# Whole-array transposes for the first four groups, two 64-row tiles for all other groups, and a rewritten work order

## The chip, the core and the metric

The kernel runs on one core of a Trainium2 chip. The metric is the device time of one execution in microseconds (us), lower is better. The engines are TensorE (PE, matrix products; its weight loads are listed apart as PEld), VectorE (DVE), ScalarE (ACT), GpSimd (POOL) and SyncE (SP, which here issues the transfers). Matrix products and transposes write to PSUM banks; the other engines read these.

## The reference, cut to what matters

`x` is 4 batches of 12480 tokens with 128 channels, `inducing` 32 rows of 128, the weights are 128 x 2048 and 2048 x 128, all float32.

```python
def mab(q, kv):
    s = scale * (q @ kv.transpose(0, 2, 1))
    s = s - s.max(-1, keepdims=True)
    a = np.exp(s)
    a /= a.sum(-1, keepdims=True) + 1e-09
    return a @ kv
h = mab(I, x)                       # 32 inducing rows attend to the tokens
attn = mab(x, h)                    # the tokens attend to the 32 rows of h
hid = attn.reshape(49920, 128) @ w_in
out = np.maximum(0.01 * hid, hid) @ w_out
```

## The kernel before

The tokens of a batch are cut into six groups of 2048 and a rest group of 192 (g = 6). A group's rows lie in SBUF as 128 partitions with 16 tokens each (`xr`, 1 MB, six buffers). Two passes run over the groups of each batch.

The first pass: LD loads a group; T (`turn`, L1711) transposes it on PE, from SBUF into PSUM, and C (`turned`, L1734) copies the four results to `xT` on ACT or DVE; S1 forms the 32 scores of each token; E takes their maxima and a copy; after two groups (a step: 0 and 1, 2 and 3, 4 to 6) RD, X and NM combine the maxima; W takes the exponentials on ACT, Y transposes them on DVE in blocks of 32; V is the value product on PE, with `xr` as its moving operand, after which `xr` is free for a later load; GA adds the steps up. After the third step ZP, RZ, HS, HP and HC make the transposed hidden state `hT`. H, HT, SH, G, FO, FC, SP and SC then fold both weight matrices and the leak into one matrix of 32 rows for the batch (`folded`).

The second pass of the same batch: S2 forms scores with `hT`, LO, LE and U make weights of them, and O, the output product, uses `folded`. SA, RC, D and DM divide by the sums, ST stores. The second pass of a batch is woven into the first pass of the next. The weights arrive in eight blocks of 0.5 MB (LW), each converted from 64 to 32 bits by CA and CT on ACT, CB and CO on DVE and CP on POOL.

What order each engine works in is written out by hand in the table `ORDER`: every token stands for one call, the letter at its end is the engine (a for ACT, v for DVE, p for POOL), the digit behind @ a PSUM bank. Each engine runs its own instructions in the order of this table and waits for others only where data or a buffer need it. SP issues all loads and stores of the table in order, too.

A transpose before the change comes in two forms. The groups in `EARLY` (all six of batch 0 and the first three of batch 1) are turned in one visit in four tiles of 32 rows, 64 PE passes with 32 columns each, into both pairs of banks (`po0`, `po1`) that the output products use later. The other fifteen are turned in two visits in two tiles of 64 rows, 16 passes with 64 columns each, into two single banks. The rest group is turned whole, in two passes with 96 rows.

Of the kernel before, what the change touches and what calls it, by code (L numbers as in the profile page):

```python
# [1383 lines left out]
class Plan:  # L1384
# [3 lines left out]
        LD0.0.0 LD0.0.1 T0.0.0 C0.0.2a C0.0.3a C0.0.0v C0.0.1v LD0.1.0 T0.1.0 C0.1.0a C0.1.1a C0.1.3v C0.1.2v LW0  # L1388
        CT0 CB0 S10.0@0 S10.1@1 CA0 E0.0 CO0 CP0 LD0.2.0 LD0.3.0 LD0.4.0 T0.2.0 C0.2.0a C0.2.1a C0.2.3a C0.2.2a LW1
        E0.1 RD0.0 X0.0@2 NM0.0 W0.1 W0.0 T0.3.0 C0.3.2v C0.3.0a C0.3.1a C0.3.3v Y0.0 Y0.1 S10.2@3 CA1 CB1 CT1 CO1  # L1390
        CP1 LW2 CA2 T0.4.0 C0.4.3a C0.4.2a C0.4.0a C0.4.1a V0.0@0 S10.3@1 LD0.5.0 V0.1 E0.2 CB2 CT2 CO2 CP2 ZT0.0
        E0.3 RD0.1 LW3 CB3 CA3 LW4 LD0.6.0 LD1.0.0 LD1.1.0 T0.5.0 C0.5.2v C0.5.0a C0.5.1a C0.5.3v S10.4@2 X0.1@3
        NM0.1 CO3 T0.6.0@1 C0.6.0v E0.4 S10.5@3 E0.5 CA4 AL0.1 S10.6@1 E0.6 RD0.2 CB4 CO4 CT3 CP3 CT4 W0.3 W0.2 CP4
        T1.0.0 C1.0.2a C1.0.1a C1.0.0a X0.2@2 NM0.2 AL0.2 W0.5 Y0.3 Y0.2 V0.2@3 V0.3 ZT0.1 Y0.5 GA0.0 W0.4 Y0.4
        C1.0.3a W0.6 ZT0.2 Y0.6 LW5 LW6 CA5 GA0.1 T1.1.0 C1.1.3a C1.1.2a C1.1.1a CA6 C1.1.0a CT5 CB5 CO5 CP5 ZP0@1
        RZ0 CB6 V0.4@2 V0.5 V0.6 GA0.2 HS0 CO6 CT6 CP6 S11.0@0 E1.0 HP0@3 HC0 LW7 CB7 S11.1@1 E1.1 CA7 CO7 RD1.0 CT7
        CP7 H0.0@2 HT0.0 SH0.0 S20.0@0 X1.0@3 NM1.0 LO0.0 LE0.0 LD1.2.0 LD1.3.0 T1.2.0 T1.3.0@12 C1.3.1v C1.2.1a
        C1.3.0a C1.2.2a U0.0 C1.2.3a C1.2.0a S20.1@3 G0.0p FO0.0@1 FC0 T1.3.1@20 C1.3.2v C1.3.3a LO0.1 LE0.1 S20.2@1
        W1.0 Y1.0 SP0@0 SC0 W1.1 U0.1 S11.2@2 E1.2 LO0.2 O0.0.0.0 SA0.0.0.0a O0.0.0.1 SA0.0.0.1a D0.0.0.0a RC0.0.0
# [958 lines left out]
```

## Time and profile before

| | before |
|---|---|
| time, median of 3 runs | 199.67 us (198.2 to 202.84) |
| the profiled execution's own time | 198.97 us |
| span from first to last instruction | 197.2 us |
| PE busy | 169.0 us (86%), 3471 products and 3471 weight loads |
| DVE busy | 146.6 us (74%) |
| ACT busy | 127.6 us (65%) |
| POOL busy | 89.8 us (46%) |
| DMA | 55.93 MB, 284 GB/s over the span |
| granted PE clock, mean | 0.913 of 2.4 GHz |

A timeline row gives the start in us from the beginning of the span, the time from the group's first start to its last end, the engine, the line of the kernel, the operation, output<-input, the shapes and how many instructions were merged into the row; in brackets stands how long the engine stood idle just before it and what ended the idle time. "issue" is idle time in which the engine waited for nothing that the profile shows. A granted clock of 1.00 is 2.4 GHz, 0.50 is 1.2 GHz. PE passes of float32 operands count double in the rows of products, single in the rows of transposes.

### The profile page before, as it was taken

How to read it: one execution, taken by the hardware profiler on the slowest of the kernel's cores; microseconds unless marked ns; L12 is line 12 of the kernel's file. 1: busy time of each engine (PE TensorE's matmuls, PEld its weight loads, DVE VectorE, ACT ScalarE, POOL GpSimd, SP SyncE). 2: the span in 40 equal slices, each digit the busy share in tenths (PEclk: the TensorE clock that was granted, in tenths of full speed). 3: DMA queues.
4: the chain of work that ended last, by engine and by line, in shares of the span. 5: the costliest groups of instructions: out<-in, count | busy, mean ns of one | idle time of the engine just before them, and what ended most of it. 6: DMA issues, size and time to landing. Idle time of an engine off the chain costs nothing.

```text
span 197.2 us, 8331 instructions
## 1 busy us (share of the span) xinstructions
PE 169.0 (86%) x3471; PEld 109.2 (55%) x3471; DVE 146.6 (74%) x461; ACT 127.6 (65%) x336; POOL 89.8 (46%) x96
## 2 busy tenths in 40 slices
PE   7596988698799999979889999799999978898930
PEld 2546664573438586766437578345683673465710
DVE  2361869859497978969659898587978879988950
ACT  2247659864697976964649986558996843666410
POOL 2010132208227386760156655284294654788640
PEclk9955589699999999999999999999999999999555
DMA  6999879599403999998995559999846353397992
GB/s 201 369 419 424 313 277 412 180 294 407 178 3 106 396 357 383 406 385 285 354 370 217 216 179 352 381 384 344 332 177 258 118 185 132 132 315 283 380 371 72
DMA packets 19357, 55.93 MB, mean 284 GB/s; under 512 B 1104, under 2 KB 3312, under 8 KB 16368
## 3 DMA queue, kind: packets, MB, share of 16 engines
q1 hardware_dynamic: 19056, 55.22, 75.3%
q8 instruction: 28, 0.46, 1.0%
q10 hardware_dynamic: 256, 0.11, 0.3%
q14 instruction: 17, 0.14, 0.2%
HBM read 29.77 MB, written 25.56 MB: 281 GB/s over the span
## 4 chain that ended last, share of the span: by engine, by line


## 5 line engine op out<-in xcount | busy, mean ns | idle before, releaser
L2052 POOL TENSOR_TENSOR osb<-stage,inv 128x512 f32<-128x512 f32 (+1 forms) x75 | 75.1, 1019 | 55.7 <-DVE inv L2033 18.8
L1741 ACT COPY xT<-xT_ps 128x512 f32<-128x512 f32 x66 | 36.7, 601 | 26.2 <-PE xT_ps L1729 26.0
L2004 PE MATMUL po<-folded,uT 32*128 32x129 f32 (+1 forms) x792 | 42.8, 302 | 2.8 <-ACT uT L1984 0.9
L2045 ACT COPY stage<-po 128x512 f32<-128x512 f32 (+1 forms) x75 | 41.5, 581 | 4.4 <-PE po L2004 4.3
L2004 PEld LDWEIGHTS po<-folded,uT 32*128 32x128 f32 (+1 forms) x792 | 32.2, 189 | 21.5 <-ACT stage L2045 7.6
L1729 PE MATMUL xT_ps<-ident,xr 32*128 32x32 f32 (+1 forms) x1056 | 36.1, 242 | 6.9 <-issue 3.2
L1729 PEld LDWEIGHTS xT_ps<-ident,xr 32*128 32x128 f32 (+1 forms) x1056 | 30.8, 157 | 19.2 <-issue 10.7
L1843 PE MATMUL h_ps<-xr,ay 128*32 128x128 f32 x768 | 27.0, 291 | 2.3 <-DVE z L1826 2.3
L1749 PE MATMUL s_ps<-xT,indT 128*32 128x512 f32 x192 | 27.6, 662 | 0.3 <-ACT cv_a L1684 0.3
L1741 DVE COPY xT<-xT_ps 128x512 f32<-128x512 f32 x30 | 19.9, 682 | 10.6 <-PE xT_ps L1729 10.6
L1749 PE MATMUL s_ps<-xT,hT 128*32 128x512 f32 x192 | 26.4, 599 | 1.6 <-issue 1.3
L1843 PEld LDWEIGHTS h_ps<-xr,ay 128*32 128x32 f32 x768 | 22.4, 117 | 4.3 <-issue 2.7
L2026 ACT ACTIVATE inv<-po 128x4 f32<-128x4 f32 (+1 forms) x75 | 11.4, 175 | 19.3 <-PE po L2004 18.8
L1984 ACT ACTIVATE uT<-s_ps,least 128x512 f32<-128x512 f32 (+1 forms) x28 | 18.2, 650 | 4.4 <-DVE least L1968 4.2
L1959 DVE TENSOR_REDUCE low<-s_ps 128x1 f32<-128x512 f32 (+1 forms) x28 | 17.1, 609 | 3.5 <-PE s_ps L1749 3.4
L1770 DVE TENSOR_SCALAR_CACHE_REDUCE e<-s_ps 128x512 f32<-128x512 f32 (+1 forms) x28 | 17.1, 614 | 3.0 <-PE s_ps L1749 2.1
L1812 ACT ACTIVATE e<-e,nm 128x512 f32<-128x512 f32 (+1 forms) x28 | 18.9, 679 | 0.7 <-DVE nm L1796 0.7
L2047 DVE TENSOR_TENSOR osb<-po,inv 128x512 f32<-128x512 f32 (+2 forms) x29 | 18.0, 629 | 1.2
L1709 POOL TENSOR_TENSOR w_in_sb<-cv_a,cv_t 128x512 int32<-128x512 int32 x4 | 5.2, 1288 | 26.7 <-DVE cv_a L1694 21.0
L1821 DVE STREAM_TRANSPOSE ay<-e 128x512 f32<-128x512 f32 (+1 forms) x28 | 17.0, 621 | 0.0
L2033 DVE RECIPROCAL inv<-inv 128x8 f32<-128x8 f32 (+1 forms) x52 | 9.9, 191 | 2.0
L1709 POOL TENSOR_TENSOR w_out_sb<-cv_a,cv_t 128x512 int32<-128x512 int32 x4 | 5.3, 1324 | 10.6 <-ACT cv_t L1700 8.2
(95 smaller groups left out, 147.1 us busy)
## 6 DMA issues: line engine op xcount, KB each, us to landing
xr<-in_x_dram SPq DMA_DIRECT2D x23, 1024.0 KB, 8.1
out_dram<-osb SPq DMA_DIRECT2D x21, 1024.0 KB, 5.8
out_dram<-osb SPq DMA_DIRECT2D x6, 512.0 KB, 4.2
raw<-in_moe_w_in_dram SPq DMA_DIRECT2D x4, 512.0 KB, 14.1
raw<-in_moe_w_out_dram SPq DMA_DIRECT2D x4, 512.0 KB, 4.7
xr<-in_x_dram SPq DMA_DIRECT2D x2, 512.0 KB, 4.2
xrr<-in_x_dram SPq DMA_DIRECT2D x4, 96.0 KB, 6.7
out_dram<-osb SPq DMA_DIRECT2D x3, 96.0 KB, 4.9
```

Of the source, the lines that this page charges most:

```text
L1729: nc.tensor.matmul(V["T", b, g, j][:, n * k : n * k + n], xr[b, g][part, 8 * q + k, :], ident[part, part], is_transpose=True, tile_positio ...
L1741: copying(engine)(xT[b, g][:, n * at : n * at + n], V.pop(("T", b, g, j))[:, :n])
L1749: nc.tensor.matmul(ps[32 * j : 32 * j + 32, :w].rearrange("p (k r) -> p k r", r=32), lhsT, tokens[:, :, 32 * j % n : 32 * j % n + 32], sta ...
L1770: nc.vector.tensor_scalar(out=e[:rows], in0=V.pop(("S", b, g))[:rows, :w], scalar1=1.0, scalar2=None, op0=ALU.mult, op1=ALU.max, accum_out ...
L1812: nc.scalar.activation(e[:rows, :w], e[:rows, :w], AF.Exp, bias=nms[b, p][:rows], scale=SCALE, accum_out=zg[:rows])
L1843: nc.tensor.matmul(hp[32 * (k % 4) : 32 * (k % 4) + 32, :], t[:rows, k, :], rows_in[:rows, k, :], start=(i == 0 and k < 4), stop=(last[k % ...
L1959: V["latest", "DVE"] = nc.vector.tensor_reduce(out=low[:rows], in_=V["S2", b, g][:rows, :w], op=ALU.max, axis=AX.X, apply_absolute_value=T ...
L1984: V["latest", "Activation"] = nc.scalar.activation(dst, src, AF.Exp, bias=least[:rows, b, g : g + 1])
L2004: V["latest", "PE"] = nc.tensor.matmul(po[:m, j % 2, (P + 1) * i : (P + 1) * (i + 1)], uT[b, g][part, columns], folded[b % 2][part, :], st ...
L2045: nc.scalar.copy(raw[:m, :nj, :n], src)
L2047: nc.vector.tensor_tensor(out=dst, in0=src, in1=inverse_of(b, g, h, t)[4], op=ALU.mult)
L2052: V["latest", "Pool"] = nc.gpsimd.tensor_tensor(out=dst, in0=raw, in1=inv, op=ALU.mult)
```

## The change

The groups 0 to 3 of batch 0 (`WHOLE`) are turned by the whole array: four visits of four passes with 128 rows and 128 columns each, one bank a visit, two visits to a pair. All other big groups are turned in two visits in two 64-row tiles, those in `EARLY` into one bank pair a visit, the rest as before. The first load, which is cut in two pieces, lets the first two visits start on its first piece. Scores read `xT` with another stride for the whole groups. `ORDER` is written anew throughout; two planning costs change with it and don't reach the program.

```diff
-        LD0.0.0 LD0.0.1 T0.0.0 C0.0.2a C0.0.3a C0.0.0v C0.0.1v LD0.1.0 T0.1.0 C0.1.0a C0.1.1a C0.1.3v C0.1.2v LW0
+        LD0.0.0 T0.0.0 T0.0.1 C0.0.1v LD0.0.1 LD0.1.0 LD0.2.0 LD0.3.0 T0.0.2 C0.0.0v T0.0.3 C0.0.2a C0.0.3a T0.1.0
...
     EARLY = [(0, g) for g in range(NG)] + [(1, g) for g in range(3)]
+    WHOLE = [(0, g) for g in range(4)]
     PIECES = {(0, 0): 2}
-    T_FOUR, T_TWO = 0.85, 0.45
+    T_WHOLE, T_TWO = 0.437, 0.52
...
-        parts = range(4) if (b, g) in EARLY else range(2 * q, 2 * q + 2)
+        whole = (b, g) in WHOLE
+        n, parts = (P, [q]) if whole else (64, [2 * q, 2 * q + 1])
         for j in parts:
             if (b, g) not in EARLY:
                 V["T", b, g, j] = one_ps("xT_ps")
...
-        n = 32 if (b, g) in EARLY else 64
         for k in range(TOK // n):
             for i, j in enumerate(parts):
                 part = slice(n * i, n * i + n)
                 nc.tensor.matmul(
-                    V["T", b, g, j][:, n * k : n * k + n], xr[b, g][part, 8 * q + k, :], ident[part, part],
+                    V["T", b, g, j][:, n * k : n * k + n],
+                    xr[b, g][part, (4 if whole else 8) * q + k, :], ident[part, part],
                     is_transpose=True, tile_position=(n * i, 0),
                 )
...
-        at = j if (b, g) in EARLY else 2 * (j % 2) + j // 2
+        at = j if g == RG or (b, g) in WHOLE else 2 * (j % 2) + j // 2
...
-            n = rows if g == RG else 32 if (b, g) in EARLY else 64
-            at = 0 if g == RG else w * j if (b, g) in EARLY else 2 * w * (j // 2)
+            n = rows if g == RG or (b, g) in WHOLE else 64
+            at = 2 * w * (32 * j // n)
...
-        visits, tiles = (1 if early or not big else 2), (4 if big else 1)
+        whole = (b, g) in WHOLE
+        visits, tiles = (4 if whole else 2 if big else 1), (4 if big else 1)
...
-            banks = [("po0", "T", b, g), ("po1", "T", b, g)] if early else [("ps", "T", b, g, j) for j in js]
+            banks = [(f"po{js[0] // 2}", "T", b, g)] if early else [("ps", "T", b, g, j) for j in js]
```

PE's order at the start of the program, before: `busy_ps` is a warm-up, `xT_ps` a turn, `s_ps` a score product, `mx_ps` the combined maxima of a step, `h_ps` a value product (x16 is one group).

```order
L1655 MATMUL ind_ps<-ident,ind 128x32
L1729 MATMUL xT_ps<-ident,xr 128x32 x128
L1749 MATMUL s_ps<-xT,indT 32x512 x8
L1729 MATMUL xT_ps<-ident,xr 128x32 x64
L1598 MATMUL mx_ps<-rd,e_77 32x8 x4
L1729 MATMUL xT_ps<-ident,xr 128x32 x64
L1749 MATMUL s_ps<-xT,indT 32x512 x4
L1729 MATMUL xT_ps<-ident,xr 128x32 x64
L1843 MATMUL h_ps<-xr,ay 32x128 x16
L1749 MATMUL s_ps<-xT,indT 32x512 x4
```

The same place on PE in the changed kernel.

```order
L1657 MATMUL ind_ps<-ident,ind 128x32
L1731 MATMUL xT_ps<-ident,xr 128x128 x32
L1752 MATMUL s_ps<-xT,indT 32x512 x4
L1731 MATMUL xT_ps<-ident,xr 128x128 x16
L1752 MATMUL s_ps<-xT,indT 32x512 x4
L1731 MATMUL xT_ps<-ident,xr 128x128 x16
L1600 MATMUL mx_ps<-rd,e_77 32x8 x4
L1752 MATMUL s_ps<-xT,indT 32x512 x4
L1731 MATMUL xT_ps<-ident,xr 128x64 x16
L1752 MATMUL s_ps<-xT,indT 32x512 x4
L1731 MATMUL xT_ps<-ident,xr 128x64 x16
L1846 MATMUL h_ps<-xr,ay 32x128 x32
```

A group of 64 passes has become one of 16 (group 4 of 32), turns and scores alternate from the first group on, the score of group 3 and the second half of group 4's turn stand ahead of the first value product, and the first two value products stand together.

DVE's order from the maxima of step 2 of batch 0 on, before: `e,rm` are the maxima of a group, `cv_b` and `cv_a` sign and join of a weight block, `ay` the transposed exponentials that a value product needs, `lower,nm` a step's minimum.

```order
L1770 TENSOR_SCALAR e,rm<-s_ps 96x64
L1779 TENSOR_TENSOR rd<-rm,own 128x12
L1688 TENSOR_SCALAR cv_b<-raw 128x512
L1694 SCALAR_TENSOR_TENSOR cv_a<-cv_a,cv_b 128x512
L1798 TENSOR_SCALAR lower,nm<-mx_ps,nm 128x12
L1821 STREAM_TRANSPOSE ay<-e 128x512 x2
```

The same place on DVE in the changed kernel.

```order
L1773 TENSOR_SCALAR e,rm<-s_ps 96x64
L1773 TENSOR_SCALAR e,rm<-s_ps 128x512
L1782 TENSOR_TENSOR rd<-rm,own 128x12
L1824 STREAM_TRANSPOSE ay<-e 128x512 x2
L1801 TENSOR_SCALAR lower,nm<-mx_ps,nm 128x12
L1690 TENSOR_SCALAR cv_b<-raw 128x512
L1696 SCALAR_TENSOR_TENSOR cv_a<-cv_a,cv_b 128x512
L1690 TENSOR_SCALAR cv_b<-raw 128x512
L1696 SCALAR_TENSOR_TENSOR cv_a<-cv_a,cv_b 128x512
```

The two transposes have moved ahead of the weight block and of the minimum.

SP's order at the start, before: `xr` is a load of x, `raw` a weight block.

```order
L1670 DMA xr<-in_x_dram 128x1024 x2
L1670 DMA xr<-in_x_dram 128x2048
L1675 DMA raw<-in_moe_w_in_dram 128x1024
L1670 DMA xr<-in_x_dram 128x2048 x3
L1675 DMA raw<-in_moe_w_in_dram 128x1024 x2
```

The same place on SP in the changed kernel.

```order
L1672 DMA xr<-in_x_dram 128x1024 x2
L1672 DMA xr<-in_x_dram 128x2048 x3
L1677 DMA raw<-in_moe_w_in_dram 128x1024
L1672 DMA xr<-in_x_dram 128x2048
L1677 DMA raw<-in_moe_w_in_dram 128x1024
```

The first weight block has moved behind the loads of groups 2 and 3, and the second and third no longer go out together.

## Rows read from the trace of the kernel before

**Rows 1.** The page: busy us (share, count) of each engine; granted clock in 40 slices.

```profile
PE 169.0 (86%) x3471; PEld 109.2 (55%) x3471; DVE 146.6 (74%) x461; ACT 127.6 (65%) x336; POOL 89.8 (46%) x96
...
PEclk9955589699999999999999999999999999999555
```

**Rows 2.** Busy time by stage: us from:to, length, busy per engine, clock, DMA share, GB/s.

```profile
9.30:26.40 17.10, 15.50 (x313) 9.96 (x313) 10.02 (x21) 10.74 (x22) 2.58 (x2) 0.51 0.94 376
26.40:36.60 10.20, 6.82 (x210) 4.50 (x205) 7.98 (x28) 7.84 (x19) 3.85 (x3) 0.99 0.92 345
...
56.30:181.00 124.70, 116.90 (x2392) 75.40 (x2391) 103.39 (x337) 90.55 (x256) 71.06 (x72) 1.00 0.75 274
```

**Rows 3.** Timeline of PE in the opening.

```profile
5.17 1.42 PE L1729 MATMUL xT_ps<-ident,xr 32*128 32x32 f32 x64
8.71 1.92 PE L1729 MATMUL xT_ps<-ident,xr 32*128 32x32 f32 x64 [2.12 <-DMA xr<-in_x_dram]
10.55 3.64 PE L1749 MATMUL s_ps<-xT,indT 128*32 128x512 f32 x16
14.13 1.92 PE L1729 MATMUL xT_ps<-ident,xr 32*128 32x32 f32 x64
...
17.21 0.32 PE L1729 MATMUL xT_ps<-ident,xr 32*128 32x32 f32 x2 [0.94 <-ACT xT L1741]
18.19 1.92 PE L1729 MATMUL xT_ps<-ident,xr 32*128 32x32 f32 x62 [0.66 <-ACT xT L1741]
...
40.09 1.18 PE L1729 MATMUL xT_ps<-ident,xr 32*128 32x32 f32 x64
41.21 0.24 PE L1598 MATMUL z_ps<-zn,e 128*32 128x1 f32 x8
...
56.33 0.74 PE L2004 MATMUL po<-folded,uT 32*128 32x129 f32 x16
```

**Rows 4.** Timeline of PE: the rows that began after an issue gap.

```profile
29.20 0.49 PE L1729 MATMUL xT_ps<-ident,xr 32*128 32x32 f32 x18 [0.49 <-issue]
...
53.98 0.34 PE L1729 MATMUL xT_ps<-ident,xr 64*128 64x64 f32 x4 [1.42 <-issue]
...
99.11 1.05 PE L1749 MATMUL s_ps<-xT,hT 128*32 128x512 f32 x3 [1.29 <-issue]
...
124.39 0.52 PE L1729 MATMUL xT_ps<-ident,xr 64*128 64x64 f32 x9 [1.25 <-issue]
...
161.99 0.42 PE L1598 MATMUL floor_ps<-ident,floor 128*32 128x128 f32 x8 [1.05 <-issue]
```

**Rows 5.** DMA queues (packets, MB, share): page; 51.5 to 54; 26.5 to 29.5 us.

```profile
q8 instruction: 28, 0.46, 1.0%
...
q8 instruction: 1, 0.02, 2.9%
...
q8 instruction: 1, 0.02, 2.1%
```

**Rows 6.** Timeline of PE: a 64-row visit and the turn of a rest group.

```profile
64.81 0.71 PE L1729 MATMUL xT_ps<-ident,xr 64*128 64x64 f32 x16
65.45 0.38 PE L1716 MATMUL xT_ps<-ident,xrr 96*128 96x96 f32 x2
65.76 1.06 PE L1749 MATMUL s_ps<-xT,hT 128*32 128x512 f32 x8
```

**Rows 7.** Timeline of DVE and PE: from step 2's maxima to the hidden state.

```profile
33.74 0.42 DVE L1688 TENSOR_SCALAR cv_b<-raw 128x512 int32<-128x512 int32 x1
...
34.26 0.69 DVE L1694 SCALAR_TENSOR_TENSOR cv_a<-cv_a,cv_b 128x512 int32<-128x512 int32 x1
...
35.02 1.30 DVE L1821 STREAM_TRANSPOSE ay<-e 128x512 f32<-128x512 f32 x2
...
36.47 3.69 PE L1843 MATMUL h_ps<-xr,ay 128*32 128x128 f32 x64 [2.34 <-DVE z L1826]
...
44.30 0.32 PE L1598 MATMUL hT_ps<-folds,hc 128*32 128x64 f32 x8
```

More of the change, by code (lines that the diff above doesn't have):

```diff
@@ L1469 @@
+        DM3.5.1.1 ST3.3 ST3.4.0 ST3.4.1 ST3.5.0 ST3.5.1 END@0 SA3.6.0.0v O3.6.0.1 SA3.6.0.1v RC3.6.0 D3.6.0.0v
+        D3.6.0.1v SI3.6 ST3.6
     """
@@ L2129, in last_of @@
         b, g = (b, g - 1) if g else (b - 1, NG)
-        parts = {"LD": (PIECES.get((b, g), 1) - 1,), "T": (0 if g == RG or (b, g) in EARLY else 1,), "O": (0 if g == RG else 1, 1)}
+        parts = {"LD": (PIECES.get((b, g), 1) - 1,), "T": (0 if g == RG else 3 if (b, g) in WHOLE else 1,), "O": (0 if g == RG else 1, 1)}
         return [(kind, b, g, *parts.get(kind, ()))]
@@ L2148, in first_pass @@
         early = (b, g) in EARLY
-        visits, tiles = (1 if early or not big else 2), (4 if big else 1)
+        whole = (b, g) in WHOLE
+        visits, tiles = (4 if whole else 2 if big else 1), (4 if big else 1)
         for q in range(visits):
             js = range(tiles * q // visits, tiles * (q + 1) // visits)
-            banks = [("po0", "T", b, g), ("po1", "T", b, g)] if early else [("ps", "T", b, g, j) for j in js]
-            add(("T", b, g, q), {"PE": (T_FOUR if early else T_TWO) if big else 0.175}, lambda _, q=q: turn(b, g, q), mode="R" if early else "H" if big else "F",
-                after=[("LD", b, g, PIECES.get((b, g), 1) - 1)] + ([("T", b, g, q - 1)] if q else last_of("T", b, g)), rank=at,
-                takes=banks + ([] if q else [(xtag, b, g)]), uses=banks + [(rtag, b, g)])
+            banks = [(f"po{js[0] // 2}", "T", b, g)] if early else [("ps", "T", b, g, j) for j in js]
+            pieces = PIECES.get((b, g), 1)
+            add(("T", b, g, q), {"PE": (T_WHOLE if whole else T_TWO) if big else 0.175}, lambda _, q=q: turn(b, g, q), mode="F" if whole or not big else "H",
+                after=[("LD", b, g, pieces - 1 if not whole else q * pieces // 4)] + ([("T", b, g, q - 1)] if q else last_of("T", b, g)), rank=at,
+                takes=([] if early and whole and q % 2 else banks) + ([] if q else [(xtag, b, g)]), uses=banks + [(rtag, b, g)])
             for j in js:
-                bank = banks[j // 2] if early else banks[j - js[0]]
+                bank = banks[0] if early else banks[j - js[0]]
                 add(("C", b, g, j), {"ACT": 0.49 if big else 0.22, "DVE": 0.61 if big else 0.27}, lambda e, j=j: turned(b, g, j, e),
-                    after=[("T", b, g, q)], rank=at, like=("C", b, g, j - 1) if early and j % 2 else None,
+                    after=[("T", b, g, q | 1 if early and whole else q)], rank=at, like=("C", b, g, j - 1) if early and j % 2 else None,
                     uses=[bank, (xtag, b, g)])
```

159 lines of the change are left out of this document (79 added, 80 removed).

## Prediction

> **What bounds the kernel now.** I read the busy shares and the slices of the span first [rows 1]. TensorE (PE) is the busiest engine, and the row of its granted clock, a digit for each 4.9 us, shows the lower level (5, that is 1.2 GHz) in slices 3 to 5 and part of slice 8. Then I read the busy times by stage [rows 2]. From 56.3 us, where the first output product starts, to 181.0 us PE is busy 116.90 of 124.70 us (94%), VectorE (DVE) 103.39 (83%), and the DMA share is 0.75: there PE sets the pace, and what the opening saves or loses is handed on to the end. In the opening no engine sets the pace all through: from 9.3 to 26.4 us PE is busy 15.50 of 17.10 us at the lower clock, from 26.4 to 36.6 us 6.82 of 10.20, less than DVE with 7.98. So I ask of each edit what it does to the time of that first output product, and then what it does to PE's idle time behind it.
>
> The timeline of PE in the opening [rows 3] shows three things. A group turned in four 32-row tiles is 64 passes. It takes 1.42 us at 5.17 us, 1.92 at 8.71, 14.13 and 18.19 us, where the clock was at 1.2 GHz (mean 0.51 from 9.3 to 26.4 us), and 1.18 at 40.09 us at 2.4 GHz. Group 3 waited twice for ScalarE (ACT) to empty the banks, 0.94 and 0.66 us. And the score product at 10.55 us runs straight on into the turn at 14.13 us without the clock rising; it is high again in the stretch from 26.4 us [rows 2].
>
> The timeline also has five places where PE stood still in the middle of a run of equal passes, put down to "issue" [rows 4]: 0.49, 1.42, 1.29, 1.25 and 1.05 us, together 5.50 us. They are no data waits: at 53.98 us the last 4 of 16 passes of one visit start 1.42 us late, with the same input. I looked at the DMA queues in stretches around two of them, and each held one packet of the instruction queue, of 16 KB [rows 5]; the page counts 28 such packets in all [rows 5], one in 7.0 us. I read the five as PE having used up its instructions before the next 16 KB had come.
>
> **The change part by part.**
>
> *Fewer passes.* Four groups go from 64 passes to 16, five from 64 to 32: 4 x 48 + 5 x 32 = 352 passes less, and as many weight loads, 704 of the 6942 instructions of the page's two PE rows (10%).
>
> *Price of a whole-array pass.* The trace has no 128-row turn. From 40.09 to 41.21 us [rows 3] 64 passes in four tiles side by side take 1.12 us: 16 in a row, 70 ns each, with 32 columns. From 64.81 to 65.45 us [rows 6] 16 passes in two tiles take 0.64 us: 8 in a row, 80 ns each, with 64 columns. Continued by columns, 128 give 100 ns, so 1.6 us for a group of 16 at 2.4 GHz. The lower bound is 80 ns (1.3 us); the upper is the pair of 96-row passes at 65.45 us, which the next row follows after 0.31 us: 155 ns (2.5 us). I take 100 ns, since two rows of the same kind carry it. At 1.2 GHz I scale by 1.92/1.18 = 1.63: 2.6 us a group.
>
> *The first four groups.* Before, 1.42 + 1.92 + 1.92 + 0.32 + 1.92 = 7.5 us. After, at the lower clock, 4 x 2.6 = 10.4 us: +2.9 us; at the higher, 6.4 us: -1.1 us. Against it the waits for ACT go (-1.6 us): a visit now fills one pair of banks while the other pair is emptied, where a 32-row group needs both pairs. I take the lower clock, as the row for 9.3 to 26.4 us has it: +1.3 us by the first value product. The bounds are 155 ns at the lower clock, 4 x 2.5 x 1.63 = 16.3 us, so +8.8 us, and 80 ns at the higher, 4 x 1.3 = 5.2 us, so -2.3 us.
>
> *Order on DVE.* The value product of step 1 starts at 36.47 us, 2.34 us after PE ran dry, and what came last is DVE [rows 7]: the sign and join of a weight block (0.42 and 0.69 us) stand ahead of the two transposes that the product needs (1.30 us from 35.02 us). The new order puts those transposes directly behind the step's maxima and products: -1.1 us. The two terms nearly cancel, and from there to the transposed hidden state at 44.30 us [rows 7] DVE is the next cover: the same joins, transposes and sums still stand ahead of it, in another order. I put the opening up to there at 0, with bounds of +8.8 - 1.6 - 1.1 = +6.1 us and -2.3 - 1.6 - 1.1 = -5.0 us.
>
> *64-row tiles for five groups.* Two visits of 0.64 us against 1.12 [rows 3, 6]: +0.16 us each. Three of them stand where PE was waiting anyway; the two that lie on the way from 44.30 us to the first output product cost 0.3 us. Group 0 of batch 1 moves behind the value product of step 1 (1.28 us), under DVE's transposes for step 2; without that cover it would cost its 1.3 us.
>
> *Instruction gaps.* The gap of 0.49 us is swallowed by the DVE chain above. The gap of 1.42 us lies between the fold and the spread that the first output product waits for, all in PE's order, so it counts in full: -1.4 us if it goes. In the new order the 32-row visits that used up instructions at 128 in 1.12 us are gone. The three later gaps (1.29 + 1.25 + 1.05 = 3.6 us) lie in visits that stay as they are; the order around them changes, and where the 16 KB boundaries then fall I can't read from a trace. Bounds: all gone, -3.6 us, or as many as before, 0. I take half, -1.8 us.
>
> *Loads.* On SP the first weight block moves behind two loads of x, the second behind one more; ACT and DVE convert them later, where they had idle time (DVE was busy 10.02 of 17.10 us from 9.3 to 26.4 us). I cost this at nothing; if the cover is gone, one block's 0.42 + 0.69 us on DVE is the price.
>
> Sum: 0 + 0.3 - 1.4 - 1.8 = -2.9 us. The profiled execution took 198.97 us (span 197.2 and 1.8 around it): 196.1 us. It lies 0.7 us below the median of the three runs; I stay close to the sum and forecast **196.0 us**.
>
> A rule speaks against the change. From 8.71 to 16.05 us turns and scores follow each other [rows 3], and the clock did not rise. The Trainium skill ("TensorE: Matmul & The Clock Gate", Part 4) says that the higher clock doesn't engage for PE transposes. By that rule, the trace agrees, longer turns delay the rise: that is the second rival, which is priced from rows alone.
>
> **The rivals.**
>
> *1. The clock stays high from the start.* The turns of group 0 now last longer, and the first four groups follow each other with fewer holes; PE idled 2.12 us before 8.71 us, and the clock fell soon after. If it doesn't fall, PE's work from 9.3 to 26.4 us (15.50 us busy) shrinks towards 15.50/1.63 = 9.5 us, and DVE, with 10.02 us in the same stretch, becomes the bound of it. Of the 6.0 us I let three quarters through, 4.5: 196.1 - 4.5 = 191.6 us. For it: PE idles less before the clock fell. Against it: transposes ran there before, too, and it fell.
>
> *2. The clock rises later.* Whole-array turns take 10.4 us of the opening, and before the rise came with the value product. If it is still low up to 36.6 us, the 6.82 us of PE work between 26.4 and 36.6 us become 6.82 x 1.63 = 11.1: +4.3 us, and with the +1.3 us of the longer turns no longer covered 196.1 + 5.6 = 201.7 us. It decides the sign once PE does about 5 us of work at the lower clock behind the first value product (5 x 0.63 = 3.2, more than the gain of 2.9). For it: the rows on the clock; against it: PE no longer pauses between 8.7 us and the first value product.
>
> *3. The gaps only move.* The order is different, the fetch boundaries fall elsewhere, and as many visits run dry, in the opening too. 198.97 + 0.3 = 199.3 us. For it: all three later gaps are in 64-row turns, scores and floor products [rows 4], which remain. The Trainium skill ("Runtime: NRT & Kernel Launch", Instruction fetch mechanics) calls the cost of crossing such a 16 KB boundary mostly hidden. The trace agrees for most of the 28 packets, since only five gaps stand beside them.
>
> **How the numbers follow.** Forecast 0.38, rival 1 0.27, rival 2 0.20, rival 3 0.15. A difference of 2% (4.0 us on the median of 199.67) is about what a measurement of this kernel can tell from no change: faster means under 195.7 us, slower over 203.7 us. The forecast's own range is 196.0 with half of the later gaps either way and 1 us of the opening, 193.2 to 198.8; 0.14 of it counts as faster, the rest, 0.24, as the same. Rival 1 is faster (0.26 of 0.27). Rival 2 is slower in four of ten cases, where no later gap goes either (0.08), and the same in six (0.12). Rival 3 is the same, with 0.02 slower. Together: faster 0.40, same 0.24 + 0.01 + 0.12 + 0.13 = 0.50, slower 0.10. To leave out no more than 2 in 10, the range goes from 189.5 (rival 1 with all later gaps gone) to 202.0 us.
>
> **What would show it.** Right: turns of the first groups of about 100 ns a pass at 2.4 GHz or 165 ns at 1.2 GHz; no gap inside a visit before the first output product; that product about 1 to 2 us earlier than 56.33 us; one or two issue gaps behind it. Wrong: a granted clock of 1.00 from 5 to 26 us (rival 1), or of 0.50 beyond 30 us (rival 2); issue gaps that still add up to 5 us (rival 3); or a first output product at the old time with PE idle elsewhere in front of it, which would mean that DVE or the weight blocks, moved behind the loads of x, took the place of the gap.

## The result and the profile after

The changed kernel takes 190.95 us (median of 4 runs, 190.70 to 193.34) against 200.8 us of the kernel before in the runs beside it (198.2 to 202.84). The ratio is 0.963, with a 95% interval of 0.951 to 0.975: faster by 3.7%. The time lies in the predicted range, 5 us below the predicted value and 0.7 us from what the first rival gave (191.6). Executions of one kernel differ by up to 3.4% here, disturbed ones are left out of all ratios, and the profiles of the experiments e2, e3b, e7 and e11 are of disturbed executions, so that of these only single rows are used.

| | before | after |
|---|---|---|
| time of the profiled execution | 198.97 us | 193.34 us |
| span | 197.2 us | 191.5 us |
| first value product starts | 24.00 us | 20.66 us |
| value product of step 2 (groups 2 and 3) starts | 36.47 us | 29.95 us |
| transposed hidden state starts | 44.30 us | 40.50 us |
| first output product starts | 56.33 us | 51.02 us |
| from there to the end of the span | 140.87 us | 140.48 us |
| issue gaps of PE in that stretch | 4.30 us | 0.77 us |
| PE's waits for loads of x in that stretch | none | 2.90 us |

The profiled execution is the slowest of the four, and two things that it shows at 30 and 94 us are the reason to look at it closely. First the page: busy time and granted clock, which answer to [rows 1].

```profile
PE 166.3 (87%) x3119; PEld 106.8 (56%) x3119; DVE 148.8 (78%) x460; ACT 128.1 (67%) x338; POOL 90.3 (47%) x97
...
PEclk9999996999999999999979999999999999999855
```

The 352 passes are gone (3471 to 3119), but PE's busy time fell by only 2.7 us. The long stretch of the lower level in slices 3 to 5 is gone as well; in the opening one slice (the seventh, 28.7 to 33.5 us) is below full, and a smaller dip follows behind 94 us. By stage, to be held against [rows 2]; the third stretch is again 124.7 us from the first output product on:

```profile
9.30:26.40 17.10, 15.92 (x241) 10.31 (x242) 12.60 (x32) 10.61 (x22) 2.58 (x2) 1.00 1.00 380
26.40:36.60 10.20, 6.80 (x150) 5.63 (x144) 9.24 (x29) 8.72 (x23) 4.45 (x3) 0.83 0.97 361
51.00:175.70 124.70, 118.04 (x2380) 75.49 (x2376) 103.44 (x334) 92.05 (x260) 70.43 (x73) 0.99 0.77 274
```

From 9.3 to 26.4 us the granted clock is 1.00 where it was 0.51, and DVE does 12.60 us of work where it did 10.02: the kernel is further along. The DMA share is 1.00, so in this stretch the loads are now at their limit. PE's timeline in the opening, to be held against [rows 3, 7]:

```profile
5.41 2.31 PE L1731 MATMUL xT_ps<-ident,xr 128*128 128x128 f32 x16
8.99 1.94 PE L1731 MATMUL xT_ps<-ident,xr 128*128 128x128 f32 x16 [1.27 <-DMA xr<-in_x_dram]
10.86 1.06 PE L1752 MATMUL s_ps<-xT,indT 128*32 128x512 f32 x8
...
20.66 1.95 PE L1846 MATMUL h_ps<-xr,ay 128*32 128x128 f32 x64
...
28.73 0.25 PE L1600 MATMUL mx_ps<-rd,e 128*32 128x12 f32 x8 [1.67 <-DVE rd L1782]
29.95 3.59 PE L1846 MATMUL h_ps<-xr,ay 128*32 128x128 f32 x64 [0.96 <-DVE lower L1801]
...
35.35 0.71 PE L1731 MATMUL xT_ps<-ident,xr 64*128 64x64 f32 x16 [0.50 <-ACT xT L1744]
36.33 0.71 PE L1731 MATMUL xT_ps<-ident,xr 64*128 64x64 f32 x16 [0.27 <-ACT xT L1744]
...
40.50 0.32 PE L1600 MATMUL hT_ps<-folds,hc 128*32 128x64 f32 x8 [0.51 <-DVE hc L1874]
...
51.02 0.74 PE L2007 MATMUL po<-folded,uT 32*128 32x129 f32 x16
```

The first turn takes 2.31 us; the second takes 1.87 us from its start to the next row, 117 ns a pass. One group's scores take 1.06 us, where two took 3.64 before. The row at 29.95 us has the same 64 products as the one at 20.66 us and takes 3.59 us instead of 1.95: after two waits of 1.67 and 0.96 us PE runs at its lower speed once more. On DVE, behind the minimum that this product waited for, stands a long join of a weight block:

```profile
31.67 1.59 DVE L1696 SCALAR_TENSOR_TENSOR cv_a<-cv_a,cv_b 128x512 int32<-128x512 int32 x1
```

The value product of step 2 starts 6.5 us earlier than before, the hidden state only 3.8 us: 2.7 us are handed back. PE's rows say where. In the new order one more group's turn stands between the two (35.35 and 36.33 us, some 1.3 us of work); PE waits 0.77 us for ACT to empty the banks of these turns and 0.51 us for DVE, where another join stands ahead of `hc`. The joins themselves are largely hidden here behind the slow value product; where that product is fast (e8, below), PE waits for DVE instead. The next 1.5 us are won behind the hidden state, where the gap of 1.42 us in [rows 4] has gone. Behind the first output product PE's waits have changed in kind:

```profile
75.55 0.71 PE L1731 MATMUL xT_ps<-ident,xr 64*128 64x64 f32 x16 [0.65 <-DMA xr<-in_x_dram]
...
94.11 0.71 PE L1731 MATMUL xT_ps<-ident,xr 64*128 64x64 f32 x16 [2.25 <-DMA xr<-in_x_dram]
...
108.02 0.27 PE L1731 MATMUL xT_ps<-ident,xr 64*128 64x64 f32 x1 [0.40 <-issue]
...
118.67 0.72 PE L2007 MATMUL po<-folded,uT 32*128 32x129 f32 x10 [0.37 <-issue]
```

The gaps are down to 0.77 us. Before, they came to 4.30 us in this stretch: the three in [rows 4] and a fourth that the prediction had overlooked.

```profile
85.56 0.21 PE L1598 MATMUL mx_ps<-rd,e 128*32 128x8 f32 x4 [0.71 <-issue]
```

In their place stand 2.90 us of waiting for loads of x. SP's own rows show why the later one has so little time:

```profile
77.61 8.49 SPq L2068 DMA_DIRECT2D out_dram<-osb  x3
86.20 1.86 SPq L1672 DMA_DIRECT2D xr<-in_x_dram  x2
```

SP spends 8.49 us on three stores, which wait for their results, and only then issues the two loads, though their buffers had come free with value products around 80 us. That leaves the load short of time but doesn't settle that PE waits: e5 issues the same loads at the same 86.20 us and has no such wait.

### The profile page after: what moved, and what is told of

It reads as the page before. It is cut to its first block, busy times and chain, and to the rows that moved or that the text cites. A ratio compares the mean times of both kernels' runs of the same rounds, so it can differ in the third digit from the quotient of the medians.

```text
span 191.5 us, 7623 instructions
## 1 busy us (share of the span) xinstructions
PE 166.3 (87%) x3119; PEld 106.8 (56%) x3119; DVE 148.8 (78%) x460; ACT 128.1 (67%) x338; POOL 90.3 (47%) x97
## 4 chain that ended last, share of the span: by engine, by line
## 5 line engine op out<-in xcount | busy, mean ns | idle before, releaser
L2055 POOL TENSOR_TENSOR osb<-stage,inv 128x512 f32<-128x512 f32 (+1 forms) x77 | 75.9, 1006 | 57.3 <-ACT stage L2048 24.2
L1744 ACT COPY xT<-xT_ps 128x512 f32<-128x512 f32 x64 | 35.5, 594 | 22.6 <-PE xT_ps L1731 22.2
L2048 ACT COPY stage<-po 128x512 f32<-128x512 f32 (+1 forms) x77 | 42.6, 574 | 5.5 <-PE po L2007 5.2
L1731 PE MATMUL xT_ps<-ident,xr 64*128 64x64 f32 (+1 forms) x704 | 36.1, 233 | 6.5 <-DMA xr<-in_x_dram 4.7
L1731 PEld LDWEIGHTS xT_ps<-ident,xr 64*128 64x128 f32 (+1 forms) x704 | 30.3, 139 | 18.3 <-issue 7.6
L1846 PE MATMUL h_ps<-xr,ay 128*32 128x128 f32 x768 | 25.7, 286 | 1.0 <-DVE lower L1801 1.0
L1752 PE MATMUL s_ps<-xT,indT 128*32 128x512 f32 x192 | 25.9, 628 | 0.0
L1744 DVE COPY xT<-xT_ps 128x512 f32<-128x512 f32 x32 | 21.0, 681 | 6.3 <-PE xT_ps L1731 6.3
L1752 PE MATMUL s_ps<-xT,hT 128*32 128x512 f32 x192 | 25.3, 599 | 0.0
L1696 DVE SCALAR_TENSOR_TENSOR cv_a<-cv_a,cv_b 128x512 int32<-128x512 int32 x8 | 7.6, 946 | 1.9 <-ACT cv_a L1686 1.6
```

The source lines that it names most:

```text
L1731: nc.tensor.matmul(V["T", b, g, j][:, n * k : n * k + n], xr[b, g][part, (4 if whole else 8) * q + k, :], ident[part, part], is_transpose= ...
L1744: copying(engine)(xT[b, g][:, n * at : n * at + n], V.pop(("T", b, g, j))[:, :n])
L1752: nc.tensor.matmul(ps[32 * j : 32 * j + 32, :w].rearrange("p (k r) -> p k r", r=32), lhsT, tokens[:, :, 32 * j % n : 32 * j % n + 32], sta ...
L1846: nc.tensor.matmul(hp[32 * (k % 4) : 32 * (k % 4) + 32, :], t[:rows, k, :], rows_in[:rows, k, :], start=(i == 0 and k < 4), stop=(last[k % ...
L2048: nc.scalar.copy(raw[:m, :nj, :n], src)
L2055: V["latest", "Pool"] = nc.gpsimd.tensor_tensor(out=dst, in0=raw, in1=inv, op=ALU.mult)
```

## The experiments

All experiments but e3, e3b and e4 start from the changed kernel; those three start from the order of the kernel before. Where a diff shows other tiles, the visits in `ORDER` that go with them are left out. Speed is read from the scores of one group (8 rows): 1.05 us at the higher speed, 1.93 at the lower.

**e1: the new order with the old 32-row tiles for the first four groups.**

```diff
-    WHOLE = [(0, g) for g in range(4)]
+    WHOLE, QUARTERS = [], [(0, g) for g in range(4)]
```

> The changed kernel with its order and its 64-row tiles, but the first four groups turned again in four 32-row tiles (64 passes a group, one visit). Theory clock (the whole-array turns are what keeps the TensorE clock at 2.4 GHz in the opening): the granted clock falls to 0.5 from about 9 us on, as in the kernel before; the first output product comes 3 to 6 us later than 51.0 us, and the time is 194 to 197 us. Rival order (the new order alone keeps PE supplied, so the clock stays up whatever the tiles): clock 1.00 from 9 to 26 us, first output product at 50 to 52 us, time 190 to 192 us, like the changed kernel.

Measured: 196.73 us, ratio 0.994 (0.986 to 1.001). First the stretch 9.3 to 22 us, then PE's timeline:

```profile
9.30:22.00 12.70, 12.67 (x244) 7.35 (x248) 7.19 (x16) 6.07 (x13) 0.57 (x1) 1.00 1.01 400
```

```profile
9.33 2.05 PE L1735 MATMUL xT_ps<-ident,xr 32*128 32x32 f32 x64 [1.65 <-DMA xr<-in_x_dram]
11.31 1.94 PE L1756 MATMUL s_ps<-xT,indT 128*32 128x512 f32 x8
...
53.37 0.74 PE L2011 MATMUL po<-folded,uT 32*128 32x129 f32 x16
...
72.91 0.40 PE L1735 MATMUL xT_ps<-ident,xr 64*128 64x64 f32 x5 [2.21 <-issue]
...
87.19 0.43 PE L1850 MATMUL h_ps<-xr,ay 128*32 128x128 f32 x8 [2.31 <-issue]
```

Turns of 1.92 to 2.05 us and scores of 1.94 are the lower speed, and it lasts to 24 us. Yet the granted clock of the stretch reads 1.00. The trace's own list of clock changes says why: in e1 its first entry is a rise at 24.5 us, and the time before a first entry reads 1.00. The warm-up of the changed kernel reads so too, and its four rows take 3.78 us where four rows of the same size take 1.98 in e4. So PE did not fall in e1, it had never risen; in the kernel before it rose at 5.7 us and fell at 9.1, in the changed one it rose at 6.2. By durations the theory holds: in the new order, too, PE runs at the lower speed with the old tiles, although from 9.3 us on it does nothing but work (12.67 of 12.70 us), and with these tiles the new order is worth nothing that can be told from no change. The first output product comes 2.4 us later than in the changed kernel, and behind it two gaps of 4.52 us in sum have come back: the order by itself does not keep them away.

**e2: the first four groups in two 64-row tiles.**

```diff
-    WHOLE = [(0, g) for g in range(4)]
+    WHOLE = []
```

> The changed kernel with its order, but the first four groups in two visits of two 64-row tiles (32 passes a group). Theory clock: between the two forms; if what counts is how much of the array a pass fills, the clock falls for at least part of 9 to 26 us, and the first output product comes 1 to 5 us later than 51.0 us (192 to 196 us). Rival order: clock 1.00 and first output product at 50 to 52 us, 190 to 192 us.

Measured: 193.38 us, ratio 0.967 (0.953 to 0.980).

```profile
9.12 1.21 PE L1735 MATMUL xT_ps<-ident,xr 64*128 64x64 f32 x32 [1.46 <-DMA xr<-in_x_dram]
...
18.84 0.71 PE L1735 MATMUL xT_ps<-ident,xr 64*128 64x64 f32 x16 [2.48 <-DMA xr<-in_x_dram]
```

From the second group on the turns take 1.21 us a group, less than the whole-array ones, at the higher speed, and the first output product starts at 49.95 us. PE waited 1.46 us in front of the second group and 2.48 us at 18.84 us and stayed fast. So the whole-array form is not needed, and a pause alone doesn't always lower the speed. As with e1, two long gaps (2.49 and 1.08 us) stand behind the first output product.

**e3: the new tiles in the old order, and e3b: the same with 32-row tiles left for the other five groups.** Edit in the old `ORDER` (e3b only the first line pair, and `QUARTERS` holds the five groups):

```diff
-T0.0.0
+T0.0.0 T0.0.1 T0.0.2 T0.0.3
...
-T0.4.0
+T0.4.0 T0.4.1
```

> The order of the kernel before with the new tiles: the first four groups whole (their four visits together where the one visit stood), the other five early groups in two 64-row visits. Theory clock: the clock is 1.00 from 9 to 26 us in the old order too; PE gains some 4 us there, the weight block stays ahead of the transposes on DVE, first output product at 52 to 54 us, time 193 to 196 us. Rival order: the clock falls to 0.5 as before, the longer turns cost 1 to 3 us, time 199 to 202 us. On the instruction gaps: if it is the 32-row visits that run out of instructions, gaps of PE put down to issue add up to under 2 us; if they depend on where in the program the fetch boundaries fall, they move and can be as large as before (5.5 us).

> The order of the kernel before, its 32-row tiles for five early groups, and only the first four groups turned whole. Theory clock: clock 1.00 from 9 to 26 us and a gain of some 4 us in the opening, as with the 64-row tiles; the time differs from the run with both by under 1 us unless instruction gaps differ. Rival order: no gain, 199 to 202 us.

Measured: e3 193.08 us, ratio 0.976 (0.967 to 0.985); e3b 193.84 to 199.46 us, for which no ratio is given. In e3:

```profile
9.27 1.94 PE L1736 MATMUL xT_ps<-ident,xr 128*128 128x128 f32 x16 [1.23 <-DMA xr<-in_x_dram]
...
32.63 1.95 PE L1851 MATMUL h_ps<-xr,ay 128*32 128x128 f32 x64 [1.90 <-DVE z L1834]
...
48.98 0.74 PE L2012 MATMUL po<-folded,uT 32*128 32x129 f32 x16
...
114.50 0.84 PE L2012 MATMUL po<-folded,uT 32*128 32x129 f32 x11 [2.29 <-issue]
```

The tiles alone bring the whole gain of the opening: the first output product starts at 48.98 us, 7.4 us earlier than in the kernel before and even earlier than with the new order. The value product of step 2 still stands behind the joins (32.63 us), but between the first turn and the first output product no work runs at the lower speed. Whether the 64-row form of the other five groups matters was to come out of e3b; its runs spread over nearly 3% and leave that open.

**e4: the kernel before, with PE's wait of 2.12 us filled by two products of zeros.**

```diff
-LD0.1.0 T0.1.0
+LD0.1.0 FILL0@2 T0.1.0
...
+        for _ in range(2):
+            nc.tensor.matmul(ps[:, :512], idle[:, :P], idle[:, :512], start=True, stop=True)
```

> The kernel before, unchanged in order and tiles, with two products of zeros (512 columns each, thrown away) put into PE's wait of 2.12 us for the second group's load. It asks whether that wait or the 32-row turn lets PE fall to its lower speed. The clock is to be read from the duration of a group's scores: 1.05 us for 8 rows at the high speed, 1.93 at the low one. Theory wait: PE doesn't stand still, stays at the high speed, the turns of groups 1 to 3 take 1.18 us instead of 1.92 and the first score products 1.05 a group; the first output product comes 3 to 5 us earlier than 56.33 and the time is 193 to 196 us. Theory tile (32-row passes lower the speed even without a pause): the second group's turn and the scores run at the low speed as before, the first output product stays at 55.5 to 57 us, 198 to 200 us.

Measured: 199.45 us, ratio 1.002 (0.996 to 1.008).

```profile
8.50 1.33 PE L1735 MATMUL xT_ps<-ident,xr 32*128 32x32 f32 x64
...
12.93 1.18 PE L1735 MATMUL xT_ps<-ident,xr 32*128 32x32 f32 x64 [0.66 <-DMA xr<-in_x_dram]
...
16.52 1.31 PE L1735 MATMUL xT_ps<-ident,xr 32*128 32x32 f32 x64 [1.52 <-DMA xr<-in_x_dram]
17.75 1.78 PE L1756 MATMUL s_ps<-xT,indT 128*32 128x512 f32 x8
...
36.31 3.64 PE L1850 MATMUL h_ps<-xr,ay 128*32 128x128 f32 x64 [2.34 <-DVE z L1833]
```

Neither theory had it. The turns of groups 1 to 3 are fast, as the theory of the wait says, but a faster PE in the old order only runs into the loads (0.66 and 1.52 us), falls to the lower speed at 17.75 us after these waits, and does later work there (the value product of step 3 takes 3.58 us, before 1.93). The gap of 1.42 us in front of the first output product is gone, and one of 1.43 us stands at 22.49 us. The first output product stays at 56.76 us. Higher speed early in the opening is worth nothing where the next wait takes it.

**e10: e1 with its wait filled in the same way** (two products of 384 columns ahead of `T0.1.0`).

```diff
-T0.1.0
+FILL0@2 T0.1.0
```

> The new order with the first four groups in 32-row tiles, as in the earlier run of 196.73 us (where scores took 1.93 us a group from 11.3 to 22 us), and PE's wait of 1.65 us for the second group's load filled with two products of zeros (384 columns, thrown away). Theory pause: without the pause PE stays at the higher speed; turns of groups 1 to 3 take 1.2 us and scores 1.05 us a group up to 22 us, and the first output product comes 1 to 3 us earlier than 53.4 us. Theory tile: 32-row turns lower the speed by themselves: group 1's turn or scores may still be fast behind the filler, but those of groups 2 and 3 take 1.9 us again, and the first output product moves by under 1 us.

Measured: 192.36 us, ratio 0.956 (0.946 to 0.965).

```profile
7.21 2.93 PE L2295 MATMUL fill_ps<-w_out_sb 128*128 128x384 f32 x4
10.07 1.44 PE L1735 MATMUL xT_ps<-ident,xr 32*128 32x32 f32 x64
11.43 1.07 PE L1756 MATMUL s_ps<-xT,indT 128*32 128x512 f32 x8
...
17.18 1.04 PE L1756 MATMUL s_ps<-xT,indT 128*32 128x512 f32 x8
...
51.99 0.74 PE L2011 MATMUL po<-folded,uT 32*128 32x129 f32 x16
```

The filler itself still runs at the lower speed (the warm-up's products of 512 columns took 3.78 us at that pace). The next turn takes 1.44 us, the two after it 1.53 and 1.85, and from the first of them on scores take 1.04 to 1.07 us, with the old 32-row tiles. So at these tiles PE stays at the higher speed once it is there; what e1 lacked was work that raised it, and its 12.7 us of 32-row turns and scores didn't. The filler both closes the pause and is whole-array work itself, and this run doesn't say which of the two counts. The first output product comes 1.4 us earlier than in e1 although a gap of 1.09 us and a slow value product (3.48 us) fell into this opening. The other 2.8 us between the spans of the two runs lie behind the first output product, where the gaps fell differently.

**e5: the changed kernel without the two warm-up products.**

```diff
-        busy = one_ps("busy_ps", 0)
-        for _ in range(2):
-            nc.tensor.matmul(busy, idle[:, :P], idle, start=True, stop=True)
```

> The changed kernel without the two warm-up products of zeros ahead of the first turn. Theory turns: whole-array turns by themselves bring PE to the high speed: the first group's 16 passes take 3.1 us or more, those of the second or third group 1.9 as in the changed kernel, and the time is 191 to 193 us. Rival warm-up: the turns only hold a speed that the warm-up had raised; without it PE stays at the low speed (16 passes in 3 us or more, scores 1.93 us a group) until the first value product at 22 to 27 us, and the time is 194 to 198 us.

Measured: 190.95 us (188.90 to 194.59), the same median as with them; no ratio is given.

```profile
4.89 3.68 PE L1733 MATMUL xT_ps<-ident,xr 128*128 128x128 f32 x16 [0.55 <-DMA xr<-in_x_dram]
8.72 2.41 PE L1733 MATMUL xT_ps<-ident,xr 128*128 128x128 f32 x16 [0.16 <-DMA xr<-in_x_dram]
11.06 1.07 PE L1754 MATMUL s_ps<-xT,indT 128*32 128x512 f32 x8
```

The first 16 passes are slow (3.68 us), the next 16 partly (2.41), and from 11.06 us on scores take 1.07 us; only the value product of step 2 is slow again, as in the changed kernel (3.59 us at 30.08 us). Before 11.06 us PE had done nothing but one small turn and whole-array transposes. So these bring the higher speed by themselves. (In e9, below, again without the warm-up, the first turn takes 3.29 us and the second already 1.94.) The Trainium skill ("TensorE: Matmul & The Clock Gate", Part 4) says that the higher clock doesn't engage for PE transposes; these rows say otherwise, and the measurement decides.

**e6: 64 passes (128 instructions) more, thrown away, in the changed kernel's wait of 1.27 us.**

```diff
-T0.1.0
+FILL0@0123 T0.1.0
```

> The changed kernel with 64 more passes on PE (identity turned in four 32-row tiles, thrown away; 128 instructions) in PE's wait of 1.27 us for the second group's load. It moves every later fetch boundary of PE by half of 256 instructions. Theory position: issue gaps of over 0.4 us stand at other places than 108.0 and 118.7 us, always at the same remainder of PE's instruction count by 256, in dense work (the value products near 80, 116 or 153 us), and their sum is not the 0.77 us of the changed kernel but 1 to 6 us. Rival order: the written order itself spaces dense visits, so gaps stay under 1 us in sum wherever the boundaries fall. If gap time comes through to the end, the time grows by the sum of the gaps beyond 0.77 us; if other waits give it back, it stays at 190.5 to 192 us.

Measured: 195.31 us, ratio 0.979 (0.973 to 0.985).

```profile
70.53 0.40 PE L1736 MATMUL xT_ps<-ident,xr 64*128 64x64 f32 x5 [2.06 <-issue]
...
84.79 0.43 PE L1851 MATMUL h_ps<-xr,ay 128*32 128x128 f32 x8 [2.29 <-issue]
```

The first output product starts at 51.14 us, as in the changed kernel; the gaps of 0.40 and 0.37 us are gone and two of 4.35 us in sum have come, at other places. Counted in the trace, PE's instruction number at the end of every issue gap of 0.35 us and more, in all kernels of this study, counting weight loads, products and semaphore steps, leaves the same remainder by 256, to within two (193: 961, 1985, 3265, 3777, 4801 and 6337 before, 2241 and 2753 here), and each ends 2.2 to 2.7 us after the start of a 16 KB instruction packet. Of the places that the expectation had named (near 80, 116 and 153 us) only the first came near. Not every boundary costs, only those whose packet is late: in the changed kernel most boundaries without a gap are crossed 2.6 to 7.7 us after the start of their packet. By the ratios the kernel is 1.7% slower than the changed one, and its gaps are 3.6 us longer than those in that one's profile. The two profiled spans differ by only 0.6 us, since the changed kernel's holds 2.90 us of load waits and this one none; how gaps and load waits come through together is in the table at the end of this section.

**e8: two loads ahead of two stores.**

```diff
-V1.4@1 U0.6
+V1.4@1 LD2.4.0 U0.6
...
-V1.5 V1.6 GA1.2
+V1.5 V1.6 LD2.5.0 GA1.2
...
-LE1.2 LD2.4.0 LD2.5.0 T2.4.0@32
+LE1.2 T2.4.0@32
```

> The changed kernel with two loads of x (groups 4 and 5 of batch 2) issued ahead of the stores of groups 5 and 6 of batch 0, directly behind the value products that free their buffers. Theory load queue: the waits of PE for loads of x behind the first output product (2.25 us at 94.1 us) go, and the time falls by 1 to 2 us below the changed kernel's 190.95, to 189 to 190 us. Rival: another wait (DVE's low, a store's buffer, POOL) takes the place, and the time stays at 190.5 to 191.5 us.

Measured: 190.40 us, ratio 0.956 (0.948 to 0.964).

```profile
29.97 1.96 PE L1851 MATMUL h_ps<-xr,ay 128*32 128x128 f32 x64 [0.96 <-DVE lower L1806]
...
39.55 0.32 PE L1605 MATMUL hT_ps<-folds,hc 128*32 128x64 f32 x8 [0.92 <-DVE hc L1879]
...
50.10 0.74 PE L2012 MATMUL po<-folded,uT 32*128 32x129 f32 x16
...
74.17 0.71 PE L1736 MATMUL xT_ps<-ident,xr 64*128 64x64 f32 x16 [0.19 <-DMA xr<-in_x_dram]
```

In e5, where the loads stand behind the stores as in the changed kernel, the turn that waited 2.25 us there waits for ACT alone:

```profile
92.13 0.71 PE L1733 MATMUL xT_ps<-ident,xr 64*128 64x64 f32 x16 [0.32 <-ACT uT L1989]
```

The load waits are down from 2.90 to 0.19 us, but gaps of 0.74, 0.71 and 0.65 us have come up. That the edit took the load wait away isn't shown, since e5 is without it too (0.42 us of load waits in all). The interval overlaps that of the changed kernel, so that a gain of its own isn't shown. The value product at 29.97 us, behind the same waits, is fast here (1.96 us), and the first output product comes 0.9 us earlier: that is what the slow one cost. The rest of the 1.6 us is lost to waits for DVE, 1.25 us at 34.31 us and 0.92 us in front of the hidden state, each behind a join of a weight block.

**e9: e8 and e5 together** (both edits above).

> The changed kernel with both edits that cost nothing so far: no warm-up products, and two loads of x ahead of two stores. If load waits and instruction gaps add up one to one behind the first output product (137.3 us with 0.6 us of them, 138.1 with 2.3, 140.5 with 3.7, 141.0 with 4.4), and eight instructions less leave the gaps where they are, the stretch is 137 to 138.5 us and the time 189 to 190 us. If other waits fill in whatever is taken away, it stays at 190.5 to 191.5 us.

Measured: 191.88 us, ratio 0.954 (0.944 to 0.964): no better than either alone. Gaps of 0.86 and 1.75 us stand behind the first output product (50.20 us), beside 0.51 us for a load; the stretch is 139.8 us, above the 137 to 138.5 expected. With eight instructions less than e8 the gaps are others; whether that is due to the instructions or to the execution isn't shown, for e11, with the changed kernel's instructions, has 1.47 us at a place where that one's profile has 0.37.

**e7: on DVE, the weight block again ahead of the two transposes.**

```diff
-RD0.2 X0.2@3 W0.2 Y0.3 Y0.2 NM0.2 LW3 CT2 CT3 CB3 CA3 CO3 CP3
+RD0.2 X0.2@3 W0.2 NM0.2 LW3 CT2 CT3 CB3 CA3 CO3 Y0.3 Y0.2 CP3
```

> The changed kernel with one thing of the old order put back on DVE: sign and join of a weight block (0.42 and 0.69 us) stand again ahead of the two transposes that the value product of step 2 (groups 2 and 3) needs. Theory term: that product, which starts at 29.95 us in the changed kernel, starts 1.1 to 2.3 us later, and the first output product follows by as much. Theory cover (the prediction's: DVE does the same work anyway up to the hidden state): the product starts later, but the transposed hidden state and the first output product stay within 0.5 us of where they were (40.5 and 51.0 us; 39.6 and 50.1 us where PE keeps its higher speed), and the time is that of the unchanged kernel within 1 us.

Measured: 193.99 us, ratio 0.961 (0.952 to 0.970).

```profile
31.27 3.38 PE L1851 MATMUL h_ps<-xr,ay 128*32 128x128 f32 x64 [2.83 <-DVE ay L1829]
...
52.29 0.74 PE L2012 MATMUL po<-folded,uT 32*128 32x129 f32 x16
```

The value product starts 1.3 us later than in the changed kernel, the first output product as well (52.29 against 51.02 us, both with a slow value product). In this execution PE had reached the step's maxima 0.5 us earlier (28.19 against 28.73 us), so from there on the old place of the weight block costs 1.9 us. The term is real and nothing covers it. The time itself can't be told from the changed kernel's.

**e11: the changed kernel once more** (same instructions, with the tile forms read from a table).

```diff
-        whole = (b, g) in WHOLE
+        n = form(b, g)
```

> The changed kernel once more (same instructions, its tile forms read from a table), for a second profile beside the others. If the two things that made its profiled execution longer than its median, the value product at the lower speed at 30 us (3.59 us) and the wait of 2.25 us for a load at 94 us, belong to the kernel, they are there again; if they are chance, the span is 188.5 to 189.5 us, with the first output product near 50 us.

Measured: 193.40 us (189.75 to 195.46).

```profile
30.26 3.16 PE L1851 MATMUL h_ps<-xr,ay 128*32 128x128 f32 x64 [0.96 <-DVE lower L1806]
...
94.05 0.71 PE L1736 MATMUL xT_ps<-ident,xr 64*128 64x64 f32 x16 [1.75 <-DMA xr<-in_x_dram]
```

Both features come back in a second profile, so they are not a single accident, but neither is there every time: the value product is fast in e8 and e9, whose instructions up to that point are the same but for the warm-up, and e5 has no such wait for a load.

**The stretch behind the first output product, taken together.** For the seven profiles in the new order other than those of e2, e7 and e11, the sum of PE's issue gaps and load waits in it, and its length:

| | gaps and load waits | first output product to end |
|---|---|---|
| e5 | 0.63 us | 137.25 us |
| e10 | 2.04 us | 138.61 us |
| e8 | 2.29 us | 138.10 us |
| e9 | 3.12 us | 139.80 us |
| changed kernel | 3.67 us | 140.48 us |
| e6 | 4.35 us | 140.96 us |
| e1 | 4.52 us | 141.43 us |

3.9 us more of such waits make 4.2 us more of time: they count nearly one to one. Not all of that need be the waits themselves. In five of the seven, all but e5 and e8, a stretch with a granted clock of 0.50 follows behind one of them (in the changed kernel from 94.9 to 98.3 us, behind the wait of 2.25 us), and what it adds isn't told apart here. In the old order the three profiles (4.30 us and 140.87 before, 2.29 and 141.42 in e3, 4.19 and 141.64 in e4) don't lie on one line, and what the new order itself is worth in this stretch stays open between 0 and some 2.5 us.

## Why the prediction was right and where it was wrong

The range held, but the gain in the opening came from a rival's mechanism, not from the forecast's own. That the median lies 0.7 us from rival 1's value is in part luck: in the profiled execution the opening, the gap in front of the first output product and the stretch behind it gave -3.8, -1.5 and -0.4 us, where rival 1 has -4.2, -1.4 and -1.8.

**The step that failed: "I take the lower clock, as the row for 9.3 to 26.4 us has it".** It carried the old tiles' speed over to the new tiles. The clock was 1.00 from 9 to 26 us, as named for rival 1, with scores at 1.06 us. The four turns cost 8.0 us, little more than the 7.5 of the old ones, while the scores between them took 1.06 us a group instead of 1.82. Instead of +1.3 us the first value product came 3.3 us earlier. The argument noted against rival 1, that transposes had run there before and the speed fell, was the error: it took turns of different tiles for one kind of work. Whole-array turns raise the speed by themselves (e5), 64-row turns go on at the higher speed through pauses of 1.46 and 2.48 us (e2), and the old 32-row turns, without a pause, don't raise it (e1) but go on at it where a filler has raised it (e10). The argument noted for rival 1, fewer pauses, isn't what these runs show: the form of the turn is. What the pause of 2.12 us did in the kernel before, where the speed rose at 5.7 us and fell at 9.1, stays open; e4, which fills it, keeps the speed only until the loads make PE wait again.

**Price of a whole-array pass.** 100 ns were taken from the series of columns; 117 ns were measured, inside the bounds of 80 and 155. It does little harm, since the loads are at a DMA share of 1.00: with e2's shorter turns PE waits for loads instead, and its first value product starts at 21.12 us, no earlier.

**Order on DVE.** The move was worth 1.9 us from the step's maxima on (e7), 1.1 were predicted. But "DVE is the next cover" was half right: 6.5 us at the value product of step 2 became 3.8 us at the hidden state. In the profiled execution that is one more group's turn on PE (1.3 us, the price that the prediction had named for group 0 of batch 1 without cover), 0.8 us of waits for ACT and 0.5 us for DVE; in e8, with the fast value product, PE does wait for DVE, 2.2 us. Putting the opening at 0 was therefore wrong by its size: it moved by -3.8 us up to the hidden state, inside the bounds of +6.1 and -5.0 that stood beside it.

**64-row tiles.** +0.3 us was too small to be seen, and e3b doesn't settle it.

**Instruction gaps.** The gap of 1.42 us in front of the first output product went, and the hidden state's 3.8 us became 5.3: right in full. Of the later ones I had listed 3.6 us and overlooked 0.71. "Half gone" was too little for the profile (4.30 to 0.77 us), and the net was too much for it: 2.90 us of load waits took the place, so that the stretch gained 0.4 us instead of 1.8. This execution is 2.4 us longer than the median, whose stretch wasn't profiled. The reading of the gaps as late 16 KB packets was right (e6), and rival 3 was right about their nature: with other counts of instructions they come back to 4.4 or 4.5 us in the same order (e6, e1). That the changed kernel has few of them is, as far as these runs show, where its count of instructions happens to fall, not the spacing of its visits.

**Loads.** They were costed at nothing. In the opening that held but for short waits. Behind the first output product it did not: in the profiled execution PE waited 2.25 us at 94 us for one of the two loads behind three stores on SP, and 1.75 us in e11; in e5, with the same order on SP, it did not wait there. The prediction looked only at the first rows of SP's order.

**What the gain rests on.** e3 shows that the tiles alone bring the opening; e10 that a faster PE with the old tiles comes as far by its ratio (0.956), though part of its distance from e1 is gaps; e1 that the order without it brings nothing that can be measured. The new order with the new tiles is by its ratio another 1.3% below e3; the two intervals overlap, and this study can't split that between order and gaps.

## What to carry to other kernels

Where a stretch runs at the lower speed, ask what PE did just before it fell, and price a change of its work there at both speeds: a denser form of the same work, or a filler in a pause, can be worth more than the passes that a change removes, as long as the next wait (here the loads, e4) doesn't take it back. Read the speed from the duration of a row of known size as well as from the granted clock. In a PE-bound stretch, issue gaps at instruction boundaries and load waits together add to the time nearly one to one, and the gaps move with any change in the number of instructions, so a difference of 2% between two programs can be this alone; compare the gaps before crediting an edit.

## What was not expected of the hardware

- The granted clock of e1 reads 1.00 from 9.3 to 22 us while scores take 1.94 us a group, nearly twice their 1.05 us: the trace's list of clock changes begins there with a rise at 24.5 us, and before a first entry the clock reads 1.00 at the lower speed too, there as over the changed kernel's warm-up.
- Whole-array transposes alone bring PE to the higher speed: 3.68 us for the first 16 passes, 1.07 us for the first scores (e5).
- The same value product behind the same two waits (1.67 and 0.96 us) runs at the higher speed in some executions (1.96 us in e8) and at the lower in others (3.59 us in the changed kernel); the difference at the first output product is 0.9 us.
- PE's issue gaps end where its instruction count leaves one fixed remainder by 256, and with 128 instructions more at the start there were 4.35 us of them instead of 0.77. The Trainium skill ("Runtime: NRT & Kernel Launch", Instruction fetch mechanics) gives blocks of 16 KiB, or 256 instructions, with which the trace agrees, and calls the crossing mostly hidden: true of most boundaries here, but two of them cost 2.06 and 2.29 us (e6).
